# Six loads of a scan-and-adapter kernel, each issued as two transfers of unequal row counts

## The chip, the core and the metric

The kernel runs on one core of a Trainium2 chip. The core has a matrix engine (PE, with weight loads shown as PEld), a vector engine (DVE), an activation engine (ACT), a general engine (POOL), a sequencer that issues transfers (SP), and 16 DMA engines that move data between the chip's memory (HBM) and the on-chip memory (SBUF, 128 partitions). The metric is the device time of one execution in microseconds; lower is better. Before the change the median of three runs is 204.86 us (204.76 to 204.96).

## The reference

First a linear recurrence along time, one for each of 8 batches and 128 channels, then a mixture of eight small adapters on each of its 51,200 output rows, with the two largest gates out of eight:

```python
for t in range(S):                       # S = 6400, arrays (8, 6400, 128), float32
    h = a[:, t] * h + b[:, t]
    out[:, t] = h
...
logits = x @ w_gate                      # x: (51200, 128), w_gate: (128, 8)
topk = np.argpartition(-logits, K, axis=1)[:, :K]      # K = 2
...
z = x[mask] @ A[e]                       # (128, 16)
delta[mask] += w[mask, k, None] * (z @ B[e])
...
return (x + delta).astype(np.float32)
```

## The kernel before

**Tiling.** The 51,200 rows are cut into 100 units of 512 rows (`UT`). For each unit w, PE transposes a and b (`AB{w}`, into PSUM tiles pA and pB), ACT copies pA to SBUF (`aev{w}`, tile a_st), DVE runs the scan over 512 time steps (`scan{w}`, output xT, 128 channels on the partitions). Then come the logits (`L`), the products with all eight adapters' A side by side (`Z`), their weighting by the gates (`mul`, on DVE, some on POOL), a transpose back (`T`, `tev`), and the sum of x and the product with B in PSUM tile pO (`R`, `D`). `oev{v}` (line 789) copies pO into one of 24 slots of the SBUF tile outt, on ACT, in the last ten units on ACT or DVE. The gates themselves are worked out for groups of one to four units (`gating`), mostly on POOL.

**Transfers.** Loads and stores are all issued on SP, by `add_dma` (line 306 holds the `dma_start`). One load brings two neighbouring units of a or of b: 128 rows of 4 KB, one row for each partition, 512 KB in all. Row p of the load holds 8 consecutive time steps, so the lower 64 partitions hold one unit and the upper 64 the other. Only the loads of a0, b0, b1 and a99 bring one unit (256 KB, rows of 2 KB). The loads of a start at the odd units, those of b at the even ones. a_in and b_in are rings of eight such loads; a load into a slot waits until the units that used it have been transposed. 49 stores write two units each (512 KB) and two write one (256 KB). A store waits for the copies of its units, and up to unit 75 also for the scan 20 units later (`HOLD`, `FREE`), so stores trail behind.

**Landing.** Every transfer adds 16 to a semaphore of its slot; `add_dma` counts 16 for each transfer in its list `starts` and the users wait for the sum. So a load of two transfers is used when both have landed.

**Order.** `_Plan.schedule` is a planner in the host program: it simulates the engines with the costs that are written beside each operation, takes at each step the engine that can go on soonest, and on it the ready operation with the smallest key (its unit plus an offset for its kind). The result is a fixed order of instructions for each engine. For a transfer it takes 450 ns on SP for each `dma_start`, then a time on a link that transfers share one after the other: 1265 ns for a load of two units. `load` (line 417) gives a load the key w - 16, so loads go ahead of stores when both are ready.

**What the change touches.** The call of `add_dma` inside `load`, whose fourth argument is the list of transfers, and a new table of constants at the top.

Of the kernel before, what the change touches and what calls it, by code (L numbers as in the profile page):

```python
# [20 lines left out]
POOL_MULS = (0, 20, 4, 2)  # L21
HOLD = 20
FREE = 96
RING = 8
XR = 16
NOUT = 24
# [60 lines left out]
class _Plan:  # L87
# [9 lines left out]
    def add(self, name, eng, kind, unit, cost, emit, deps=(), dma=None, bank=None, mode=None):  # L97

        engs = (eng,) if isinstance(eng, str) else eng
        cost = cost if isinstance(cost, dict) else {e: cost for e in engs}  # L100
        self.ops[name] = _Op(name, engs, kind, unit, cost, emit, list(deps), dma, bank, mode)
# [98 lines left out]
def bass_associative_scan_2x2__then__mixture_of_adapters_kernel(  # L200
# [20 lines left out]
    lo, hi, every, at = POOL_MULS  # L221
# [23 lines left out]
    with ExitStack() as stack:  # L245
# [11 lines left out]

        a_in = sb(nc.sbuf_tensor("a_in", [128, RING, QI * D], F32))
        b_in = sb(nc.sbuf_tensor("b_in", [128, RING, QI * D], F32))
        a_st = [sb(nc.sbuf_tensor(f"a_st{i}", [128, UT], F32)) for i in range(2)]  # L260
# [36 lines left out]
        def add_dma(name, eng, unit, starts, slot, time, deps=()):  # L297

            if slot not in dma_sem:
                dma_sem[slot] = [sb(nc.semaphore("q_" + "_".join(map(str, slot)))), 0]  # L300
            dma_sem[slot][1] += 16 * len(starts)
            sem, value = dma_sem[slot]

            def emit(h):
                for dst, src in starts:
                    last = h.dma_start(dst, src).then_inc(sem, 16)
                return last

            add(name, eng, "dma", unit, (450.0 * len(starts), 0.0), emit, deps, (sem, value, time))
# [91 lines left out]
        def place(t, w):  # L401

            shift = 1 if t == "a" else 0
            half = 64 * ((w + shift) % 2)
            return (w + shift) // 2, slice(half, half + 64)
# [7 lines left out]
        def column(t, w):  # L413

            return w * UT if t == "b" else 0

        def load(t, w):

            n = place(t, w)[0]
            many = 1 if (t, w) in alone else 2  # L420
            dst, i = rings[t][:, n % RING, :], QI
            if many == 1:
                dst, i = dst[:, column(t, w) : column(t, w) + UT], Q
            src = rows_of[t][w * UT : (w + many) * UT, :].rearrange("(p i) d -> p (i d)", i=i)
            for k in range(many):
                load_of[t, w + k] = f"ld{t}{w}"
            add_dma(
                f"ld{t}{w}",
                "sp",
                w - 2 * RING + (0 if w > 3 else -200),  # L430
                [(dst, src)],
                (t, n % RING, many, w if many == 1 else 0),
                650.0 if many == 1 else 1265.0,
                users.get((t, n - RING), []),
            )
# [369 lines left out]
        def store(j):  # L805
# [9 lines left out]
                632.0 * n,  # L815
                [f"oev{v}" for v in range(u0, u0 + n)] + [f"scan{u0 + HOLD}"] * (u0 + HOLD < FREE),
            )

        for w in range(NU):
            for t in "ab":  # L820
                if (t, w) not in load_of:
                    load(t, w)
# [69 lines left out]
```

## Time and profile before

| | |
|---|---|
| median of the runs | 204.86 us |
| the profiled execution | 204.77 us |
| its span, first to last instruction | 203.0 us |
| granted clock of PE, mean | 0.982 |
| moved by DMA | 79.35 MB, 391 GB/s over the span |
| read from HBM, written | 52.56 MB, 26.21 MB |
| loads of 512 KB, a and b | 49 and 49, 13.6 and 13.4 us from issue to landing (median) |
| stores of 512 KB | 49, 13.2 us (median) |

How to read the views. A stretch row gives, for a window of the execution, the busy time and the number of instructions of each engine, PE's granted clock, the mean share in which the 16 DMA engines were busy, and what they moved. A timeline row gives start, length, engine, line, operation and tiles; "SPq" is the issue of a transfer, not the transfer. A row by tile gives the shortest, median and longest duration in ns and the first and last start, and a line below it the time from issue to the landing of all of a transfer. A wait row names who waited, for whom, for how long in total, how often, and the longest.

Both kinds of work run all the time: PE is busy for 93% of the span, and the 16 DMA engines are at or above nine tenths in all but the first and the last few of 40 slices. Latencies of 13 us for a transfer whose bytes take 1.3 us on 16 engines say that some ten transfers stand in the queues.

### The profile page before, as it was taken

How to read it: one execution, taken by the hardware profiler on the slowest of the kernel's cores; microseconds unless marked ns; L12 is line 12 of the kernel's file. 1: busy time of each engine (PE TensorE's matmuls, PEld its weight loads, DVE VectorE, ACT ScalarE, POOL GpSimd, SP SyncE). 2: the span in 40 equal slices, each digit the busy share in tenths (PEclk: the TensorE clock that was granted, in tenths of full speed). 3: DMA queues.
4: the chain of work that ended last, by engine and by line, in shares of the span. 5: the costliest groups of instructions: out<-in, count | busy, mean ns of one | idle time of the engine just before them, and what ended most of it. 6: DMA issues, size and time to landing. Idle time of an engine off the chain costs nothing.

```text
span 203.0 us, 8739 instructions
## 1 busy us (share of the span) xinstructions
PE 189.5 (93%) x3594; PEld 167.2 (82%) x3594; DVE 183.8 (91%) x260; ACT 172.8 (85%) x379; POOL 115.4 (57%) x240
## 2 busy tenths in 40 slices
PE   7788899998999999999999999999999999999970
PEld 2567788887889989988899889999998999889960
DVE  1599988999999999999999999999999999999960
ACT  2357498896979999999999999999999999898870
POOL 1326767655758565646656665575775654555610
PEclk9999699999999999999999999999999999999996
DMA  7999999999999999999999999999999999999884
GB/s 184 403 408 407 406 409 402 405 407 408 407 410 413 408 413 416 404 411 408 412 408 415 408 410 409 408 413 411 410 410 411 408 414 409 400 403 358 319 318 151
DMA packets 29671, 79.35 MB, mean 391 GB/s; under 512 B 3648, under 2 KB 3776, under 8 KB 29632
## 3 DMA queue, kind: packets, MB, share of 16 engines
q1 hardware_dynamic: 28304, 78.65, 98.3%
q8 instruction: 29, 0.48, 0.9%
q10 hardware_dynamic: 1328, 0.14, 0.5%
q14 instruction: 10, 0.08, 0.1%
HBM read 52.56 MB, written 26.21 MB: 388 GB/s over the span
## 4 chain that ended last, share of the span: by engine, by line
PE 85%; ACT 7%; DVE 2%; issue 2%
PE pA L81 28%; PE pO L77 22%; PE pTL L81 14%; PE pZ L77 11%; PE pTL L77 5%; PE pB L81 4%; ACT a_st L474 3%; PE pB L77 2%; DVE xT L493 2%; ACT zwT L750 2%; ACT outt L789 2%; ACT z_sb L698 1%; DVE outt L789 0%; ACT g L667 0%; DVE warm_t L355 0%
## 5 line engine op out<-in xcount | busy, mean ns | idle before, releaser
L493 DVE TENSOR_TENSOR_SCAN xT<-a_st,xT,pB 128x512 f16<-128x512 f32 x96 | 120.2, 1252 | 4.5 <-PE pTL L77 1.0
L474 ACT COPY a_st<-pA 128x512 f32<-128x512 f32 x100 | 60.9, 609 | 19.0 <-PE pB L81 15.3
L81 PE MATMUL pA<-ident_f,a_in 64*128 64x64 f32 (+1 forms) x792 | 72.1, 231 | 2.8 <-ACT a_st L474 1.2
L81 PE MATMUL pB<-ident_f,b_in 64*128 64x64 f32 (+1 forms) x792 | 72.6, 231 | 0.2
L81 PEld LDWEIGHTS pA<-ident_f,a_in 64*128 64x128 f32 (+1 forms) x792 | 58.0, 140 | 12.6 <-ACT a_st L474 2.9
L789 ACT COPY outt<-pO 128x512 f32<-128x512 f32 x95 | 59.6, 628 | 1.6 <-PE pO L77 1.4
L81 PEld LDWEIGHTS pB<-ident_f,b_in 64*128 64x128 f32 (+1 forms) x792 | 58.1, 140 | 0.7 <-issue 0.5
L750 ACT COPY zwT<-pTL 128x512 f16<-128x512 f16 x95 | 58.0, 611 | 0.2
L712 DVE TENSOR_TENSOR zw<-pZ,g 128x512 f16<-128x512 f32 x80 | 53.5, 672 | 0.8 <-PE pTL L81 0.2
L77 PE MATMUL pO<-ident_h,xT 128*128 128x128 f16 x400 | 38.6, 220 | 0.7 <-issue 0.3
L77 PE MATMUL pZ<-cst_h,xT 128*128 128x128 f16 x400 | 38.8, 221 | 0.1
L81 PE MATMUL pTL<-ident_h,zw 128*128 128x128 f16 x380 | 38.0, 223 | 0.5 <-issue 0.3
L77 PE MATMUL pO<-cst_h,zwT 128*128 128x128 f16 x400 | 38.1, 217 | 0.3 <-ACT zwT L750 0.3
L712 POOL TENSOR_TENSOR zw<-z_sb,g 128x512 f16<-128x512 f32 x20 | 21.3, 1063 | 17.2 <-PE pTL L77 15.0
L77 PEld LDWEIGHTS pO<-ident_h,xT 128*128 128x128 f16 x400 | 27.8, 114 | 1.8 <-issue 0.6
L77 PE MATMUL pTL<-cst_h,xT 128*128 128x8 f16 x400 | 27.2, 174 | 1.8 <-DVE xT L493 1.8
L77 PEld LDWEIGHTS pZ<-cst_h,xT 128*128 128x128 f16 x400 | 28.2, 114 | 0.4 <-issue 0.3
L81 PEld LDWEIGHTS pTL<-ident_h,zw 128*128 128x128 f16 x380 | 21.9, 98 | 7.0 <-ACT zwT L750 0.7
L77 PEld LDWEIGHTS pTL<-cst_h,xT 128*128 128x128 f16 x400 | 23.3, 116 | 2.7 <-DVE xT L493 2.2
L608 POOL TENSOR_TENSOR d<-Lg,m 128x128 f32<-128x128 f32 (+3 forms) x29 | 10.8, 374 | 25.1 <-DVE m L601 25.1
L77 PEld LDWEIGHTS pO<-cst_h,zwT 128*128 128x128 f16 x400 | 24.0, 97 | 0.9 <-PE pO L77 0.6
L643 POOL TENSOR_SCALAR pn<-d 128x128 f32<-128x128 f32 (+3 forms) x31 | 17.5, 565 | 2.7
(35 smaller groups left out, 137.0 us busy)
## 6 DMA issues: line engine op xcount, KB each, us to landing
a_in<-in_a_dram SPq DMA_DIRECT2D x49, 512.0 KB, 13.6
b_in<-in_b_dram SPq DMA_DIRECT2D x49, 512.0 KB, 13.4
out_dram<-outt SPq DMA_DIRECT2D x49, 512.0 KB, 13.2
a_in<-in_a_dram SPq DMA_DIRECT2D x2, 256.0 KB, 8.0
b_in<-in_b_dram SPq DMA_DIRECT2D x2, 256.0 KB, 4.2
out_dram<-outt SPq DMA_DIRECT2D x2, 256.0 KB, 4.6
cst_f<-in_moe_A_dram ACTq DMA_DIRECT2D x1, 64.0 KB, 3.9
cst_f<-in_moe_B_dram ACTq DMA_DIRECT2D x1, 64.0 KB, 5.0
```

The costliest lines, as they stand in the source:

```text
L77: return self.h.matmul(*args, **kw)
L81: return self.h.transpose(*args)
L474: lambda h: h.copy(a_st[w % 2][:, :], pA[0][:, :]),
L493: last = h.tensor_tensor_scan(out=x_at(lo, hi), data0=a_st[w % 2][:, lo:hi], data1=pB[w % 2][:, lo:hi], initial=init, op0=ALU.mult, op1=AL ...
L608: lambda h: h.tensor_tensor(out=v(d1[s]), in0=v(Lg[s]), in1=bc(m1[s]), op=ALU.subtract),
L643: lambda h: h.tensor_scalar(v(pn[s]), v(d2[s]), 0.0, -1.0e30, ALU.is_lt, ALU.mult),
L698: lambda h: h.copy(src[:, :], pZ[v % NZ][:, :]),
L712: lambda h: h.tensor_tensor(out=oview, in0=zview, in1=gview, op=ALU.mult),
L750: lambda h: h.copy(zwT[v % 2][:, :], t_dst(v)),
L789: return copy(outt[:, v % NOUT, :], pO[v % NO][:, :])
```

## The change

A table names six loads by tensor and first unit and gives a number of rows. Each of these loads is issued as two transfers, first the rows up to that number and then the others, into the same places; the bytes, the ring slots and what waits for the load stay the same. The semaphore of the load now counts 32, and the planner takes 900 instead of 450 ns on SP for it, with the same 1265 ns on the link.

| load | units | rows | issued before at (us) |
|---|---|---|---|
| b 26 | 26, 27 | 120 + 8 | 25.25 |
| a 45 | 45, 46 | 120 + 8 | 58.45 |
| b 64 | 64, 65 | 120 + 8 | 94.46 |
| b 88 | 88, 89 | 104 + 24 | 141.87 |
| a 91 | 91, 92 | 88 + 40 | 147.15 |
| b 94 | 94, 95 | 120 + 8 | 153.63 |

```diff
@@ -21,6 +21,7 @@
 POOL_MULS = (0, 20, 4, 2)
 HOLD = 20
 FREE = 96
+FIRST_ROWS = {("b", 26): 120, ("a", 45): 120, ("b", 64): 120, ("b", 88): 104, ("a", 91): 88, ("b", 94): 120}
 RING = 8
 XR = 16
 NOUT = 24
@@ -424,11 +425,13 @@
             src = rows_of[t][w * UT : (w + many) * UT, :].rearrange("(p i) d -> p (i d)", i=i)
             for k in range(many):
                 load_of[t, w + k] = f"ld{t}{w}"
+            first = FIRST_ROWS.get((t, w))
+            starts = [(dst[lo:hi], src[lo:hi]) for lo, hi in ((0, first), (first, 128))] if first else [(dst, src)]
             add_dma(
                 f"ld{t}{w}",
                 "sp",
                 w - 2 * RING + (0 if w > 3 else -200),
-                [(dst, src)],
+                starts,
                 (t, n % RING, many, w if many == 1 else 0),
                 650.0 if many == 1 else 1265.0,
                 users.get((t, n - RING), []),
```

## The prediction

> **What bounds the kernel now.** I read the page first, for the share of each engine, then the DMA share by stretches, then the waits, then the last issues on SP.
>
> ```profile
> span 203.0 us, 8739 instructions
> PE 189.5 (93%) x3594; PEld 167.2 (82%) x3594; DVE 183.8 (91%) x260; ACT 172.8 (85%) x379; POOL 115.4 (57%) x240
> ```
>
> PE and DVE are nearly full, so the middle of the run belongs to compute. The stretches show the DMA side (columns: stretch, length, busy time of the engines, granted clock, DMA share, GB/s):
>
> ```profile
> core 0: us, PE busy (x) PEld busy (x) DVE busy (x) ACT busy (x) POOL busy (x), PEclk, DMA share, GB/s
> 65.00:165.00 100.00, 99.47 (x2009) 90.20 (x2007) 97.88 (x129) 96.05 (x210) 62.58 (x112) 1.00 1.04 411
> 182.00:197.00 15.00, 14.52 (x236) 13.06 (x230) 13.68 (x24) 12.91 (x29) 7.53 (x21) 1.00 0.88 333
> 197.00:199.90 2.90, 0.06 (x2) 0.00 (x0) 0.00 (x0) 0.59 (x1) 0.00 (x0) 0.85 0.97 364
> 199.90:201.69 1.79, 0.00 (x0) 0.00 (x0) 0.00 (x0) 0.00 (x0) 0.00 (x0) 0.50 0.07 25
> 201.69:202.97 1.28, 0.00 (x0) 0.00 (x0) 0.00 (x0) 0.00 (x0) 0.00 (x0) 0.50 0.00 0
> ```
>
> From 65 to 165 us all 16 DMA engines are busy; full occupation reads 1.04 here, since records of neighbouring packets overlap a little. So one engine alone reads 1.04 / 16 = 0.065 and moves 411 / 16 = 25.7 GB/s. That is exactly what stands from 199.90 to 201.69: 0.07 and 25 GB/s. **One DMA engine works on alone for 1.79 us** after the other fifteen have stopped, and the kernel waits for it. Between 182 and 197 us the share is already 0.88 of 1.04: 15% of 16 engines for 15 us, some 37 us of engine time, lies idle, while this one engine has a backlog. The bytes are even, since every transfer gives each engine an equal part; this engine is simply late.
>
> That compute doesn't set the end follows from the last copy and the last stores:
>
> ```profile
> 197.10 0.59 ACT L789 COPY outt<-pO 128x512 f32<-128x512 f32 x1 [0.56 <-PE pO L77]
> ```
> ```profile
> L306 SPq DMA_DIRECT2D out_dram<-outt x1: 344/344/344, 197.7 to 197.7; - x1
> DMA to landing us min/median/max: 4.4/4.4/4.4
> ```
> ```profile
> L306 SPq DMA_DIRECT2D a_in<-in_a_dram x1: 381/381/381, 0.7 to 0.7; - x1
> DMA to landing us min/median/max: 2.9/2.9/2.9
> ```
>
> The last copy ends at 197.69, its store is issued at once and lands 4.4 us later, at 202.1. A transfer of the same 256 KB, issued at 0.7 us with nothing ahead of it, lands in 2.9. So 1.5 us of the last store's latency is backlog; by the stretches it is 1.79, which I use, as a load is not a store.
>
> Loads bind nobody after the start. The only wait for one in the whole table of waits is
>
> ```profile
> PE pA L81 <- DMA a_in<-in_a_dram: 0.2, 1, 0.2
> ```
>
> **The change, part by part.** Six loads of 128 rows (4 KB a row) become two transfers each; the bytes stay. An even transfer gives each of 16 engines 128 / 16 = 8 rows. I take it that a part of 120, 104 or 88 rows still goes in eights, on 15, 13 or 11 engines, and that the rest of 8, 24 or 40 rows goes evenly over 8, 12 or 10 engines, 1, 2 or 4 rows each. A row takes 4096 B / 25.7 GB/s = 0.159 us of one engine, eight of them 1.28 us.
>
> If the engines used are always the same ones from one end of the row of sixteen, the sums over the six are: one engine (left out by all six) loses 48 rows, -7.6 us; two lose 16 rows, -2.5 us each; one loses 8 (-1.3), one loses 6 (-1.0); the other eleven gain 2 to 10 rows, +0.3 to +1.6 us (eight of them gain 10).
>
> *The end.* If the engine that is late is the one left out, its 7.6 us are over four times the 1.79 us that it is late by; two splits would do. It then stops with the others. What is late next is the fifteen: they stop at 199.90, and the last store was issued at 197.7, which no DMA engine can change. Landing, the final wait and the end of the program follow as now, 1.28 us from the last packet to the end of the span. New span: 199.90 + 1.28 = 201.2, that is -1.8 us.
>
> *The eleven that gain.* Up to 1.6 us each, nearly all of it ahead of 165 us. The idle 37 us between 182 and 197 cover it for most: 37 / 15 = 2.5 us each on average. Without that cover an engine that had no idle time would stop at 199.90 + 1.6 = 201.5, almost where the late one stops now. I take 0.1 us for the forecast and keep 1.6 as the other end.
>
> *Issue on SP.* Six more instructions of L306. Their price lies between the rows of a free and of a full queue:
>
> ```profile
> 60.52 0.33 SPq L306 DMA_DIRECT2D b_in<-in_b_dram  x1
> 147.15 2.93 SPq L306 DMA_DIRECT2D a_in<-in_a_dram  x1
> ```
>
> The second one is the very load of units 91 and 92, and its long time is back-pressure from full queues: total DMA work isn't changed, so such a stall moves rather than grows. Behind it on SP stand the next load and the next store. I take 0.33 to 1 us apiece, at the issue only. Who could feel it: PE, by a load, or ACT, by a slot of outt that isn't stored yet. For the load of 91:
>
> ```profile
> L81 PE MATMUL pA<-ident_f,a_in x724: 221/223/366, 5.0 to 166.2; 64*128 64x64 f32 x180, 128*128 128x128 f32 x1
> ```
> ```profile
> DMA to landing us min/median/max: 14.9/14.9/14.9
> ```
>
> It is issued at 147.2 and lands at 162.1. The 724 transposes of a that start up to 166.2 are 4 + 8 x 90, units 0 to 90, so unit 91 is read later than that: over 4 us of margin against, at most, 4 more rows (0.64 us) plus one issue. If that cover were gone, PE would lose the excess directly. ACT never waits for a store in the table of waits. Near the end SP issues as soon as a copy is done, so nothing that it lost before is still felt there: this copy ends at 185.40, and its store goes at 185.42.
>
> ```profile
> 184.76 0.64 ACT L789 COPY outt<-pO 128x512 f32<-128x512 f32 x1
> ...
> 185.42 12.64 SPq L306 DMA_DIRECT2D out_dram<-outt x8
> ```
>  Price on the path: 0, worst case 6 x 0.33 = 2 us if every added issue reached the end.
>
> *The planner.* It counts 900 instead of 450 ns for these six on SP. Its loads end by the line for the transfers, whose total is the same 1265 ns, so the orders of PE, DVE, ACT and POOL should stay as they are; at most a load and a store change places on SP. Price 0; the bound is again the margin of 4 us.
>
> Sum against the profiled execution: 204.77 - 1.79 + 0.1 = 203.1. The median of the runs is 204.86, 0.09 above it; I leave the sum at **203.1**.
>
> What decides is which engine is late, and no view of the profile numbers the engines. What speaks for the one left out is that the lateness is one engine's, not spread: fifteen stop within 0.4 us of each other,
>
> ```profile
> 199.50:199.90 0.40, 0.00 (x0) 0.00 (x0) 0.00 (x0) 0.00 (x0) 0.00 (x0) 0.50 0.69 256
> 199.90:201.60 1.70, 0.00 (x0) 0.00 (x0) 0.00 (x0) 0.00 (x0) 0.00 (x0) 0.50 0.07 25
> ```
>
> and a lateness that belongs to one engine's place is likelier at an end of the sixteen than inside. I hold that for a little better than even. What adds unequal work at present are instruction fetches, one engine at a time: 29 of 16 KB,
>
> ```profile
> q8 instruction: 29, 0.48, 0.9%
> ```
>
> 0.9% of 16 x 203 us over 29 is 1.0 us each; one fetch more than the others alone makes an engine late by 1.0 us.
>
> The Trainium skill, "DMA: Bandwidth & Descriptors", section "Why a DMA increments its semaphore by 16 and not by 1", says that such a transfer uses the largest number of engines, up to 16, that divides its rows, always the lowest-numbered ones: by it the last engine is left out by all six, as in my sum, while no run here shows an uneven transfer yet. Its section "Latency and other measured facts" calls engines 7 and 15 usually slower in traces, which would be the last one (203.1) or one of the eight that gain ten rows (the third rival).
>
> **The rivals.**
>
> *Partly.* The late engine goes, but one of those that gain has no idle time and sets the end: between 203.1 and 201.5 + 1.28 + 1.77 (from span to time: 204.77 - 203.0) = 204.6, middle 203.9. For it: between 197.0 and 199.9 the share is 0.97 of 1.04, so few engines idle there. Against it: the 37 us before.
>
> *The wrong engine.* The late engine is one of the eleven that gain rows. Place: its queue, from the first split on; it is never idle, so every row shows at the end: +0.3 us (2 rows) to +1.6 us (10 rows), most likely the latter. Time 204.9 + 1.6 = 206.5, slower than before. It decides as soon as the late engine isn't among the five relieved. For it: five of sixteen are relieved, and only three by over 1.79 us. Against: the argument on the end of the row, above.
>
> *Two engines at one door.* In an even transfer every engine writes its own set of partitions; with other counts the sets shift, and two engines may write the same part of the memory, at half the pace. Place: the packets of the split loads; price up to 1.28 us per split on each engine, 7.6 us for six, half of it where engines are out of step: 3.8 + 1.6 - 1.79 = +3.6 us, 208.5. It decides from about 3.5 us of such loss. Against: the 0.97 and 1.04 of the rows above show no slow pace, but they hold even transfers only. The Trainium skill, "SBUF — State Buffer", section "Door 1: The DMA port swizzle (why `[64,N]` ≈ `[32,N]`)", gives the mapping of partitions to 16 ports by which 8 neighbouring partitions lie on two ports; no run so far shows it.
>
> *Nothing.* The division into engines isn't by eights, all sixteen still share each part, and the late one stays late: 204.9. The Trainium skill, "DMA: Bandwidth & Descriptors", section "Rules for kernel authors", calls two transfers to disjoint halves of the partitions not worth the while, since both spread over all 16 engines; that would be this case, and the traces of even transfers can't decide it.
>
> **How the numbers follow.** Forecast 0.54; partly 0.14; wrong engine 0.19; one door 0.05; nothing 0.08. Differences under 0.2% (0.4 us) can't be told from none here. Faster: 0.54 + 0.12 = 0.66. Same: 0.08 + 0.01 = 0.09. Slower: 0.19 + 0.05 and 0.01 of the rest = 0.25. The forecast's own range is 202.6 to 203.6; the range of 8 in 10 goes from 202.6 through "partly" and "nothing" into the milder half of "wrong engine", 206.0, which leaves out about 0.15.
>
> **What would show it.** Right: after the last copy the DMA share drops from about 1 to 0 at once, without a stretch of 0.07 alone; the last store lands in 2.5 to 3 us instead of 4.4; the last copy still ends near 197.7; PE, DVE and ACT keep their busy times. Wrong engine: the stretch at 0.07 grows to over 3 us. One door: packets of loads slower in the stretches after 25 and 58 us, a share of 1.04 at under 400 GB/s, and waits of PE for loads. Partly: several engines late, a share of 0.13 or more at the end. The prediction fails altogether if the last copy moves by over 0.5 us, for then the planner's order changed.

## The result, and the profile after

| | before | changed |
|---|---|---|
| median of the runs | 204.91 us (4 runs, 204.76 to 205.03) | 215.35 us (4 runs, 214.33 to 216.88) |
| the profiled execution | 204.77 us | 214.33 us |
| its span | 203.0 us | 212.5 us |
| granted clock of PE, mean | 0.982 | 0.968 |

The ratio is 1.052 (95% interval 1.045 to 1.058): the change makes the kernel slower by 5%, where I had forecast 0.9% faster. The profiled execution of the changed kernel is the fastest of its four, so what follows accounts for its 9.5 us of span and not for the 10.4 between the medians.

The page of the changed kernel, first the span, the busy times, the DMA share and what DMA moved in 40 slices of 5.3 us:

```profile
span 212.5 us, 8745 instructions
PE 190.5 (90%) x3594; PEld 168.2 (79%) x3594; DVE 184.0 (87%) x260; ACT 173.0 (81%) x379; POOL 115.0 (54%) x240
...
DMA  7999999999999999999999999999999999999991
GB/s 195 402 405 409 408 406 402 233 390 407 407 412 414 342 409 408 410 410 411 410 337 392 412 405 404 410 410 414 406 339 344 327 328 385 395 395 389 356 346 49
```

The engines do the same work in the same time (PE 190.5 against 189.5 us, DVE 184.0 against 183.8); the 9.5 us are idle time. The DMA engines are busy in all but the last slices, as before. But what they move drops in four places: to 233, 342 and 337 GB/s in one slice each, and to about 330 in four slices in a row. These are the places of the split loads, some ten microseconds after their issue. So it isn't that DMA had nothing to do; it took longer for the same bytes.

The stretches around those drops in both kernels. First the kernel before, with one more row that experiment 4 needs:

```profile
core 0: us, PE busy (x) PEld busy (x) DVE busy (x) ACT busy (x) POOL busy (x), PEclk, DMA share, GB/s
37.00:43.00 6.00, 5.72 (x118) 5.16 (x118) 6.00 (x10) 5.16 (x12) 2.75 (x5) 1.00 1.03 407
71.00:74.00 3.00, 2.93 (x60) 2.66 (x56) 3.00 (x6) 2.66 (x8) 1.82 (x4) 1.00 1.03 413
107.00:113.00 6.00, 6.00 (x128) 5.46 (x125) 6.00 (x8) 5.79 (x14) 3.44 (x7) 1.00 1.04 410
113.00:153.00 40.00, 39.95 (x806) 36.20 (x805) 39.15 (x53) 38.49 (x85) 25.56 (x45) 1.00 1.03 410
153.00:179.00 26.00, 25.81 (x520) 23.37 (x520) 25.57 (x36) 24.32 (x52) 14.04 (x27) 1.00 1.04 408
```

Then the changed kernel, with a row between two drops (43 to 71 us, at the pace of before) and the end of its span in the last two rows:

```profile
37.00:43.00 6.00, 5.72 (x115) 5.09 (x114) 5.70 (x9) 5.16 (x11) 3.12 (x7) 1.00 1.04 240
43.00:71.00 28.00, 26.11 (x526) 23.39 (x527) 26.94 (x35) 24.16 (x54) 17.39 (x32) 1.00 1.03 408
71.00:74.00 3.00, 2.95 (x62) 2.57 (x60) 3.00 (x6) 2.68 (x8) 1.56 (x4) 1.00 1.05 305
107.00:113.00 6.00, 6.00 (x130) 5.47 (x126) 6.00 (x8) 5.80 (x14) 3.58 (x8) 1.00 1.04 336
153.00:179.00 26.00, 21.76 (x389) 19.57 (x386) 19.75 (x28) 18.81 (x41) 11.11 (x21) 0.87 1.02 342
205.00:207.20 2.20, 0.00 (x0) 0.00 (x0) 0.00 (x0) 0.00 (x0) 0.00 (x0) 0.62 0.90 342
207.20:211.25 4.05, 0.00 (x0) 0.00 (x0) 0.00 (x0) 0.00 (x0) 0.00 (x0) 0.50 0.17 64
```

A share of 1.04 with 240 GB/s is the picture to learn: **the DMA engines are occupied and slow**, as if each packet had to wait at the other end. Single packets do take longer: of the packets of 4 KB that start between 37 and 43 us, the median takes 162 ns before and 294 ns in the changed kernel. Each row can be turned into lost time. Where 407 GB/s were moved before and 240 now, 1 - 240/407 = 41% of 6 us is lost, 2.46 us. The four stretches give 2.46, 0.78, 1.08 and 4.21 us, together **8.5 us**. An engine whose queue never runs empty can't make that up. The prediction had found one such engine. If it is one of those that get ten rows more, 10 x 0.159 = 1.6 us come on top, and 10.1 us stand against 9.5 measured.

That sum is an estimate, for it gives the late engine the mean loss of all sixteen, while the end of the span shows an uneven loss. From 207.20 on 0.17 of 1.04 is the work of some 2.6 engines, for 4 us, where one engine worked for 1.79. Each engine leaves a landing event for its share of a transfer; for the last store these are, in us from the start of the span:

```
before:  15 events from 200.07 to 200.23 | 202.11
changed: 11 events from 207.32 to 207.47 | 207.93 208.30 209.39 210.90 211.67
```

Where one engine was late, five are now. The last is 0.77 us behind the next, where it was 1.87, so some engine lost at least 1.1 us more than the one that was late before.

PE suffers too. Its waits between 155 and 185 us, and the last copy:

```profile
PE pA L82 <- DMA a_in<-in_a_dram: 4.0, 2, 3.4
```
```profile
204.11 0.59 ACT L792 COPY outt<-pO 128x512 f32<-128x512 f32 x1 [0.56 <-PE pO L78]
```

PE, which before waited 0.2 us for loads, now waits 4.0 us for loads of a in this stretch, 3.4 of them at once (4.4 in the whole run). In the row of 153 to 179 us the granted clock is 0.87 instead of 1.00, and the last copy ends at 204.70 instead of 197.69, 7.0 us later. So there are two candidates for what set the end: the DMA queue of the late engine, +9.5 us at the last landing, or PE, +7.0 us at the last copy. The last two stores decide between them only in part:

```profile
L307 SPq DMA_DIRECT2D out_dram<-outt x2: 881/979/1077, 203.8 to 204.7; - x2
...
DMA to landing us min/median/max: 7.0/7.1/7.3
```

The last one lands 7 us after its issue, where it took 4.4 before. On eleven engines it landed 2.6 to 2.8 us after its issue, so these had no backlog left; the last engine needed 4.2 us more than they, though PE's delay gave it 7 us to catch up.

### The profile page after: what moved, and what is told of

Read it like the earlier page. It is cut to its first block, busy times and chain, and to the rows that moved or that the text cites. A ratio compares the mean times of both kernels' runs of the same rounds, so it can differ in the third digit from the quotient of the medians.

```text
span 212.5 us, 8745 instructions
## 1 busy us (share of the span) xinstructions
PE 190.5 (90%) x3594; PEld 168.2 (79%) x3594; DVE 184.0 (87%) x260; ACT 173.0 (81%) x379; POOL 115.0 (54%) x240
## 4 chain that ended last, share of the span: by engine, by line
PE 75%; ACT 8%; DMA 8%; issue 3%; DVE 2%; SPq 0%; DVEq 0%
PE pA L82 25%; PE pO L78 19%; PE pTL L82 13%; PE pZ L78 9%; DMA a_in<-in_a_dram 8%; PE pTL L78 4%; PE pB L82 4%; ACT a_st L477 3%; ACT zwT L753 2%; DVE xT L496 2%; PE pB L78 2%; ACT outt L792 1%; ACT z_sb L701 1%; ACT g L670 0%; DVE outt L792 0%
## 5 line engine op out<-in xcount | busy, mean ns | idle before, releaser
L611 POOL TENSOR_TENSOR d<-Lg,m 128x128 f32<-128x128 f32 (+3 forms) x29 | 10.8, 372 | 27.4 <-DVE m L604 27.3
L639 POOL TENSOR_TENSOR d<-Lg,m 128x128 f32<-128x128 f32 (+3 forms) x29 | 10.8, 373 | 19.0 <-DVE m L632 19.0
```

The source lines that it names most:

```text
L611: lambda h: h.tensor_tensor(out=v(d1[s]), in0=v(Lg[s]), in1=bc(m1[s]), op=ALU.subtract),
L639: lambda h: h.tensor_tensor(out=v(d2[s]), in0=v(Lg[s]), in1=bc(m2[s]), op=ALU.subtract),
```

## The experiments

The theories, as the expectations name them: *doors* or *queue* (packets of split loads, and those beside them, take longer because several engines write the same part of the memory; the late engine's queue carries this to the end), the wrong engine (the late engine gets more rows), SP (the six further issues), and PE (the lost time near the end is PE's). All edits are to the changed kernel unless said.

**1. Same number of transfers, even ones: split by columns.**

```diff
-            starts = [(dst[lo:hi], src[lo:hi]) for lo, hi in ((0, first), (first, 128))] if first else [(dst, src)]
+            starts = [(dst[:, lo:hi], src[:, lo:hi]) for lo, hi in ((0, 512), (512, 1024))] if first else [(dst, src)]
```

> The same six loads are split into two transfers each, but by columns: 128 rows of the first 2 KB, then 128 rows of the second 2 KB. Every engine keeps its own 8 partitions. Theory DOORS (in a part with other row counts two engines write the same part of SBUF, so that their packets and those of the even transfers beside them go at half the pace): no fall of the GB/s in any stretch (over 400 from 37 to 43 us, against 240 in the changed kernel), time 204.9 +- 0.5. Theory TWO TRANSFERS (the second issue and the second landing cost): the time stays near the changed kernel's, 213 to 215. Theory FEWER ENGINES (the loss is the idle of engines that get nothing): 204.9, as doors.

Measured 205.28 us (10 runs, 205.18 to 205.37) against 204.94: ratio 1.0013 (1.0004 to 1.0023). Two of its stretches:

```profile
37.00:43.00 6.00, 5.72 (x120) 5.14 (x119) 6.00 (x9) 5.15 (x12) 2.81 (x5) 1.00 1.03 402
153.00:179.00 26.00, 25.81 (x520) 23.37 (x520) 25.57 (x37) 24.32 (x52) 13.99 (x26) 1.00 1.04 406
```

The drops to 240 and 342 are gone with the rows left whole. The six further issues, and the planner's larger cost for them, cost no more than the 0.3 us that are left (0.5 at the end of the interval). SP is out.

**2. Split by rows, but even on 16 engines: 64 + 64.**

```diff
-FIRST_ROWS = {("b", 26): 120, ("a", 45): 120, ("b", 64): 120, ("b", 88): 104, ("a", 91): 88, ("b", 94): 120}
+FIRST_ROWS = {("b", 26): 64, ("a", 45): 64, ("b", 64): 64, ("b", 88): 64, ("a", 91): 64, ("b", 94): 64}
```

> The same six loads, split by rows into 64 and 64. Each part goes on all 16 engines, 4 rows each, so no engine is left out and none gets more rows than before. DOORS: 64 neighbouring partitions lie behind half of the doors, so two engines share one in each part; stretches of 37 to 43 us and so on fall to 250 to 330 GB/s again, time 209 to 216. FEWER ENGINES or unequal rows: no loss, 204.9 +- 0.5. TWO TRANSFERS: 213 to 215.

Measured 214.54 us (213.39 to 214.65), ratio 1.0467 (1.0449 to 1.0484); its span is 211.6.

```profile
37.00:43.00 6.00, 5.83 (x112) 5.06 (x110) 6.00 (x9) 5.16 (x13) 2.86 (x5) 1.00 1.05 228
71.00:74.00 3.00, 2.94 (x66) 2.65 (x63) 3.00 (x5) 2.67 (x7) 2.19 (x5) 1.00 1.06 324
107.00:113.00 6.00, 6.00 (x124) 5.44 (x124) 5.88 (x10) 5.80 (x14) 4.40 (x8) 1.00 1.03 326
153.00:179.00 26.00, 23.50 (x462) 20.88 (x458) 23.83 (x33) 22.35 (x50) 13.33 (x25) 1.00 1.04 341
```

Here 64 rows divide by 16, so by the division that the prediction assumed no engine is left out and none gets more rows. The drops are all there: 2.64 + 0.65 + 1.23 + 4.27 = 8.8 us by the rows, and the span is 8.6 longer. So the loss doesn't come from the unequal share; it comes from which rows go together in a transfer. The changed kernel's profiled span is 0.9 us longer still, which is the side on which ten further rows of the late engine would put it. It doesn't prove them: here, with no rows added to any, eleven engines land the last store 1.0 to 4.8 us after the first five, so several engines come late without further rows.

**3. and 4. Three of the six at a time.**

```diff
# the first three alone
+FIRST_ROWS = {("b", 26): 120, ("a", 45): 120, ("b", 64): 120}
# the last three alone
+FIRST_ROWS = {("b", 88): 104, ("a", 91): 88, ("b", 94): 120}
```

> Only b26, a45 and b64 are split (120 and 8). DOORS: three falls of the GB/s, as in the changed kernel, 2.4 + 0.8 + 1.1 = 4.3 us of all the DMA engines' time. The margin of the late loads (4.6 us at the least before) shrinks to about 0.3, so PE hardly waits for loads; the lost time comes back in the tail, less what idles there (37 us of engine time, 2.3 us each): 206 to 208. If the split did cost only at the six loads themselves and not in the queue behind them: 204.9.

> Only b88, a91 and b94 are split. DOORS: the fall between 153 and 179 us stays (342 GB/s in the changed kernel, 4.2 us lost), the loads of units 91 to 98, which had 4.6 to 6 us of margin, come about when they are needed; PE waits for loads 0 to 3 us instead of some 8; time 206 to 210. If the two sets simply add, this and the run with the first three add up to +10 us over before; by the margin theory (nothing waits until 4.6 us are lost, then every us counts) the sum of the two is clearly less than +10.

Measured: the first three 209.9 us, ratio 1.0249 (1.0231 to 1.0268), span 207.7; the last three 211.32 us, ratio 1.0317 (1.0300 to 1.0334), span 209.4. The first three alone:

```profile
37.00:43.00 6.00, 5.72 (x120) 5.14 (x118) 6.00 (x9) 5.16 (x11) 3.21 (x6) 1.00 1.04 238
71.00:74.00 3.00, 2.94 (x61) 2.64 (x60) 3.00 (x7) 2.68 (x7) 1.55 (x3) 1.00 1.08 302
107.00:113.00 6.00, 6.00 (x124) 5.44 (x123) 5.87 (x10) 5.79 (x14) 4.38 (x8) 1.00 1.03 333
```

The last three alone:

```profile
113.00:153.00 40.00, 39.90 (x807) 36.26 (x808) 39.11 (x52) 38.45 (x84) 25.48 (x45) 1.00 1.04 403
153.00:179.00 26.00, 24.00 (x475) 21.54 (x473) 23.69 (x33) 22.58 (x50) 13.54 (x25) 1.00 1.03 335
```

I had expected the two to add up to clearly less than the whole, since I thought that the margin of the loads and the idle DMA time near the end would swallow a part of each. Both came out longer than the 206 to 208 and 206 to 210 us that I expected. They come to +5.0 and +6.4, that is 11.3 with the decimals kept, against 10.4 for all six. Nothing is swallowed, not even of a split load issued at 25 us, with 170 us to make up for it. By the rows the first three lose 2.49 + 0.81 + 1.13 = 4.4 us, with three further rows 4.9, and the span grows by 4.7. The last three lose 0.7 + 4.65, with seven further rows 6.4, and the span grows by 6.4.

**5. The transfers by themselves.** A kernel of loads and stores only, all computation left out: groups of seven, each on the partitions named, a wait between the groups.

```python
load("all128", 0, 128); load("low120", 0, 120); load("low64", 0, 64)
load("mid64", 32, 96);  load("mid60", 32, 92);  load("low88", 0, 88)
store("o128", 0, 128, 0);   store("o120", 0, 120, N)
store("o64", 0, 64, 2 * N); store("om64", 32, 96, 3 * N)
```

> Nothing but transfers, all computation is left out: seven loads of 128 rows of 4 KB (partitions 0 to 127), then, each group after the landing of the one before, seven of 120 rows (0 to 119), of 64 rows (0 to 63), of 64 rows (32 to 95), of 60 rows (32 to 91), of 88 rows (0 to 87); then seven stores each of 128, 120, 64 (0 to 63) and 64 (32 to 95) rows. DOORS with the mapping of the skill's page (partitions p and p+32 and 4 neighbours share one of 16 ports): 410 GB/s for 128 rows; 120 rows at half the pace, 190 to 250; 64 rows on 0 to 63 at 200 to 215 and on 32 to 95 at 400; 60 rows on 32 to 91 at 380; 88 rows at 140 to 190. The stores the same by groups. FEWER ENGINES (only the engines left out cost): 120 rows 385, both kinds of 64 rows 400, 60 rows 385, 88 rows 280.

One execution, a stretch in each group, in the order of the code:

```profile
core 0: us, POOL busy (x), PEclk, DMA share, GB/s
5.00:11.00 6.00, 0.00 (x0) 1.00 1.02 402
15.00:29.00 14.00, 0.00 (x0) 1.00 0.95 224
33.00:40.00 7.00, 0.00 (x0) 1.00 0.98 200
43.00:48.50 5.50, 0.00 (x0) 1.00 0.89 295
51.50:55.50 4.00, 0.00 (x0) 1.00 0.92 342
60.00:69.00 9.00, 0.00 (x0) 1.00 0.70 214
73.50:80.00 6.50, 0.00 (x0) 1.00 1.03 407
84.00:92.00 8.00, 0.00 (x0) 1.00 0.90 345
96.00:102.50 6.50, 0.00 (x0) 1.00 0.97 208
106.00:109.00 3.00, 0.00 (x0) 1.00 1.01 406
```

With nothing else on the chip, a load of 120 rows runs at 224 GB/s and one of 128 at 402. Sixty-four rows on partitions 0 to 63 take 16 engines and still run at half pace, 200 for the load and 208 for the store; the same 64 rows on partitions 32 to 95 store at the full 406. So it is neither the number of rows nor the number of engines, but which partitions the engines reach at the same time. The Trainium skill, "SBUF — State Buffer", section "Door 1: The DMA port swizzle (why `[64,N]` ≈ `[32,N]`)", says that within each half of 64 partitions p and p + 32 share one of 16 ports; by it rows 0 to 63 reach eight ports and rows 32 to 95 all sixteen, which agrees with 208 and 406 GB/s. It isn't the whole: the load of rows 32 to 95 ran at 295 (in single microseconds between 201 and 410), where I expected full pace, the 60 rows at 342, also below what I expected, and the 88 rows at 214 above it. A store of 120 rows reaches 345, much more than the load. What the reading direction changes stays open.

**6. and 7. Can the late engine be relieved in stores instead?** In the kernel before, the last two and the last four stores of the run are split 120 + 8, after the point where loads matter.

```diff
-                [(rows, outt[:, s0 : s0 + n, :])],
+                [(rows[lo:hi], outt[lo:hi, s0 : s0 + n, :]) for lo, hi in (((0, 120), (120, 128)) if u0 >= 98 else ((0, 128),))],
# the other: u0 >= 94
```

> The kernel before, with no load split, but the last two stores (256 KB each) issued as 120 and 8 rows. Nothing waits behind them but the end. If the engine that is late at the end (1.8 us) is the one that gets nothing of the 120 rows: it has 16 packets of 2 KB less, -1.28 us, while the others, idle there, take up to 0.7 us longer at the door: 203.6 to 204.2, faster than before. If the late engine is one that takes part in both pieces: 205.0 to 205.6.

> As the run with the last two stores, and the two stores of 512 KB before them as well (units 94 to 99 in all). The late engine would lose 48 packets of 2 KB, 3.8 us, more than its 1.8; the other engines pay the door twice for 1.3 us each, and idle for 0.6 us between two stores: end between 200.5 and 202.5 in the span, time 203.4 to 205.3 if the late engine is the one left out, over 205.5 if not.

Measured 205.31 us, ratio 1.0020 (1.0011 to 1.0029), and 205.62 us, ratio 1.0045 (1.0027 to 1.0063). Both are slower, though each such store takes eight rows from the engine that is left out. If that were the late one, even the two single stores, with 16 rows of half the length, would relieve it by 16 x 0.159 / 2 = 1.3 us. So it is hardly the late one. The landing events of experiment 6 say so directly: of the 23 for the last store, in its two pieces, 21 come up to 201.08 and two at 202.47 and 202.66. So the late engine has a share in both pieces, and the one that is left out would have a share in neither.

**8. One split load, the farthest from the end.**

```diff
+FIRST_ROWS = {("b", 26): 120}
```

> Only b26 is split (120 and 8). DOORS: the stretch from 37 to 43 us falls to 240 GB/s, 2.4 us of all engines lost; by addition with the other two (0.8 and 1.1 us) about half of the +5.0 us of the run with the first three: 207.2 to 207.6. If the cost per split is the same wherever it stands: +1.7, 206.6. If what is lost at 40 us is regained in the idle of the tail: under 205.5.

Measured 207.26 us, ratio 1.0111 (1.0096 to 1.0127), span 205.5.

```profile
37.00:43.00 6.00, 5.89 (x112) 5.11 (x111) 6.00 (x9) 5.16 (x12) 2.91 (x5) 1.00 1.04 241
```
```profile
197.61 0.58 ACT L792 COPY outt<-pO 128x512 f32<-128x512 f32 x1 [0.56 <-PE pO L78]
```

One load at 25 us costs 2.45 us of DMA time at 40 us by this row, with one further row 2.6, and the span is 2.5 us longer 160 us later. The last copy ends at 198.19, only 0.5 us later than before, so the loss doesn't travel by PE; it travels in the DMA queue. Nor is it the split load's alone: between 25 and 60 us 305 packets of 4 KB take over 220 ns, against 16 in the kernel before. The split load has 128 packets, so at least 161 of the slow ones belong to other transfers.

**9. Is there one late engine that sets the end at all?** In the kernel before, the stores of units 76 to 79 are left out, 2 x 8 x 0.159 = 2.5 us of each engine.

```diff
-            store(j)
+            if stores[j][0] not in (76, 78):
+                store(j)
```

> The kernel before with the stores of units 76 to 79 left out (two of 512 KB, 2.56 us on each DMA engine, issued at 175 and 177 us, after the last load). If the late engine sets the end, as the prediction read it, 1.79 us of the 2.56 show and then the last store does: 203.0 to 203.3. If the end hangs on the last copy and its store alone: 204.9.

Measured 203.5 us against 205.02, ratio 0.9926 (0.9912 to 0.9939). Its end, and its last store:

```profile
199.90:200.50 0.60, 0.00 (x0) 0.00 (x0) 0.00 (x0) 0.00 (x0) 0.00 (x0) 0.55 0.67 249
200.50:201.60 1.10, 0.00 (x0) 0.00 (x0) 0.00 (x0) 0.00 (x0) 0.00 (x0) 0.50 0.00 0
```
```profile
L306 SPq DMA_DIRECT2D out_dram<-outt x1: 344/344/344, 198.2 to 198.2; - x1
...
DMA to landing us min/median/max: 2.5/2.5/2.5
```

The stretch with one engine alone is gone, all sixteen landing events of the last store lie within 0.18 us (200.60 to 200.77), and 1.5 us are won; the time lies 0.2 above the 203.0 to 203.3 that I expected. So the first part of the prediction holds: one engine's backlog set the end, and the stake was about the 1.8 us that it was read as.

**10. Which engine is the late one?** In the kernel before, the two single stores of units 98 and 99 are cut into three pieces: 112 rows, which all sixteen engines share, then 7 and 9 rows, or 4 and 12.

```diff
+        cuts = {98: ((0, 112), (112, 119), (119, 128)), 99: ((0, 112), (112, 116), (116, 128))}
-                [(rows, outt[:, s0 : s0 + n, :])],
+                [(rows[lo:hi], outt[lo:hi, s0 : s0 + n, :]) for lo, hi in cuts.get(u0, ((0, 128),))],
```

> The kernel before; the last two stores (units 98 and 99) are issued in three pieces each: 112, 7 and 9 rows, then 112, 4 and 12 rows, which go by the skill's rule on the lowest 16, 7 and 9, and 16, 4 and 12 engines. The late engine's landings come 1 to 2 us after the others'. Late engine among the lowest four: three late landings and three. Among the fifth to the seventh: three and two. The eighth or ninth: two and two. One of the last four: one and one. The theory that the change gives the late engine more rows excludes the last case.

204.98 us, in one run. The last landing events of the two stores, in us from the start of the span:

```
store of unit 98 (112, 7, 9): ... 199.60 199.65 199.77 | 201.41 201.62 201.81
store of unit 99 (112, 4, 12): ... 200.61 200.72 200.78 | 202.12 202.30
```

Each store has 34 events: two at once after the issue, and 16 + 7 + 9 or 16 + 4 + 12, one for each engine that has a share. Late by 1.3 us or more are three events of the first store and two of the second: the late engine has a share in the pieces of 112, 7, 9 and 12 rows and none in the piece of four. If a piece always takes engines from the same end of the row, the late engine is the fifth, sixth or seventh of sixteen. The Trainium skill, "DMA: Bandwidth & Descriptors", section "Why a DMA increments its semaphore by 16 and not by 1", says that the lowest-numbered engines are taken; the counts agree, but these events don't show from which end. By that rule the late one is 4, 5 or 6, counted from 0. Its section "Latency and other measured facts", on which the prediction drew, has 7 and 15 as usually slower in traces, but calls this specific to transfers whose descriptors are made by software; the page of the profile has the transfers here as hardware_dynamic (q1, 98.3%), so it doesn't bear on them. If the changed kernel has the same late engine, it takes part in both transfers of all six loads and gets ten rows more, 1.6 us by the price of a row.

**11. The same rows, cut so that the largest piece lies on the good partitions.**

```diff
-... for lo, hi in ((0, first), (first, 128))] if first else [(dst, src)]
+... for lo, hi in ((32, 96), (0, 32), (96, 128))] if first else [(dst, src)]
```

> The same six loads in three pieces of 64 (partitions 32 to 95), 32 (0 to 31) and 32 rows (96 to 127), on all 16 engines each. DOORS: the 64 middle rows find 16 doors and cost nothing, the 32 others two engines to a door: about half of the loss of the halves (which cost 9.6 us): +3 to +6 us, 208 to 211, and 37 to 43 us at 290 to 350 GB/s instead of 228. If only the number of pieces counts: more than with two pieces, over 214. If unequal rows count: 204.9.

Measured 208.61 us, ratio 1.0177 (1.0161 to 1.0192), span 206.7.

```profile
37.00:43.00 6.00, 5.72 (x118) 5.08 (x115) 6.00 (x8) 5.16 (x13) 3.21 (x6) 1.00 1.04 309
71.00:74.00 3.00, 2.94 (x63) 2.56 (x61) 3.00 (x5) 2.67 (x7) 2.62 (x5) 1.00 1.02 331
107.00:113.00 6.00, 6.00 (x126) 5.44 (x125) 5.86 (x9) 5.80 (x14) 4.29 (x8) 1.00 1.04 389
153.00:179.00 26.00, 25.80 (x517) 23.30 (x515) 25.51 (x35) 24.24 (x54) 13.98 (x26) 1.00 1.04 385
```

Three transfers a load instead of two, and less than half the loss of 64 + 64: 1.44 + 0.60 + 0.31 + 1.47 = 3.8 us by the rows, span +3.7. The number of transfers isn't the cost; the place of the rows is.

**12. Queue or PE at the end of the changed kernel?** The stores of units 76 to 79 are left out, as in 9, this time of the changed kernel.

> The changed kernel with the stores of units 76 to 79 left out, issued after the last load, so that no load and no engine sees it. QUEUE (the last DMA engine's backlog sets the end, PE's 7 us of delay lie under it): -2.6 us, 212.5 to 213.0. PE (the late last copy, at 204.7 instead of 197.7, sets the end): 215.0 to 215.4, as the changed kernel.

Measured 213.62 us (212.70 to 214.42), 1.7 under the changed kernel's 215.35; to the kernel before the ratio is 1.0435 (1.0415 to 1.0454). Its last copy:

```profile
204.18 0.58 ACT L792 COPY outt<-pO 128x512 f32<-128x512 f32 x1 [0.56 <-PE pO L78]
```

The last copy ends at 204.76, where it ended at 204.70; the end still comes 1.7 us earlier. The intervals of the two ratios to the kernel before just touch (up to 1.0454 here, from 1.0452 there), so the landing events of the last store are the better evidence. Fourteen come between 207.16 and 207.31, and then two at 208.95 and 210.03. In both kernels most engines are done 2.4 to 2.8 us after the last copy; the last engine is done 4.2 us after them in the changed kernel and 2.7 here. So PE's lateness isn't what sets the end; DMA's is. The size falls short of the queue theory's 2.6 us by 0.9, in a kernel whose own runs lie 2.5 us apart; why is open.

No version that does all the work beats the kernel before (experiment 9 leaves out four units' stores).

## Why the prediction was wrong

Two steps of the forecast failed. Its sum relieved the late engine by 1.79 us, and experiments 6 and 10 show that this engine isn't the one left out. And it took a row at 0.159 us in even and uneven parts alike, with no term for slower packets, which by the stretch rows cost 8.5 us. Experiments 1, 2, 5 and 11 show that this cost follows from which rows go together in a transfer.

The books close to 0.6 us in six kernels. Loss by the stretch rows, further rows of the late engine at 0.159 us, and the measured growth of the profiled span over 203.0 us:

| kernel | rows of the stretches | further rows | sum | measured |
|---|---|---|---|---|
| one load (8) | 2.45 | 0.16 | 2.6 | 2.5 |
| 32 + 64 + 32 (11) | 3.8 | 0 | 3.8 | 3.7 |
| first three (3) | 4.4 | 0.5 | 4.9 | 4.7 |
| last three (4) | 5.3 | 1.1 | 6.4 | 6.4 |
| halves (2) | 8.8 | 0 | 8.8 | 8.6 |
| the change | 8.5 | 1.6 | 10.1 | 9.5 |

The column of further rows is an estimate. The stretch rows give the mean of sixteen engines, and by the landing events of the changed kernel the loss differs between engines by 1.1 us at least.

**What bounds the kernel: right.** One engine's backlog ends the run, and the stake was 1.5 to 1.8 us (experiment 9). The sharper reading, that the engine is never idle and so every lost microsecond of DMA shows at the end, stood in the prediction only under the rival of the wrong engine. It fits all six kernels of the table.

**"If the engine that is late is the one left out": the step that failed first.** It was chosen from where the lateness is likelier to be, "at an end of the sixteen", with no row behind it. Experiment 6 finds it in both pieces of 120 and 8 rows, and experiment 10, by the rule on the lowest-numbered engines, at the fifth to seventh place, among the eight that gain ten rows. The term of -1.79 us becomes about +1.6 us, an estimate that no run shows by itself. The rival of the wrong engine had this price; its 206.5 us lacks the larger cost.

**"Two engines at one door": right in mechanism, wrong in size and chance.** What I had listed as its mark, a share of 1.04 at under 400 GB/s, is what the rows show (240, 305, 336). I wrote 1.28 us per split and 7.6 us for six, then halved it because engines would be out of step, and gave the whole 0.05. Measured are 8.5 us for six, 1.4 a split. The halving was the mis-sized term: 7.6 + 1.6 without it and without the -1.79 is 9.2 us, against 9.5. That this comes so near is in part luck, since the first three split loads cost 2.46, 0.78 and 1.08 us and not 1.28 each. The single load of experiment 8 lost 2.45 us, about twice what its own rows would lose at half pace. Transfers beside it are slowed too, by the count of slow packets; that they meet the split load's engines at the same places in memory is argued from experiment 5, since no packet's place is on record. The evidence that I held against this rival was the pace of even transfers, which, as I wrote myself, says nothing of uneven ones.

**The eleven that gain, with the idle 37 us as their cover: wrong.** That cover exists for engines that idle. The late engine has none, and the mean loss of all sixteen was 8.5 us, where I had 1.6 us as the bound. The five late events of the last store are also what the rival "partly" had named as its mark, several engines late.

**The margin of the loads: wrong.** "Over 4 us of margin against, at most, 4 more rows (0.64 us) plus one issue" counted the load's own rows. The load of units 91 and 92, for which PE waited 3.4 us, was issued at 154.09 instead of 147.15 and landed at 172.53 instead of 162.03: 6.9 of the 10.5 us were lost before its issue, the other 3.6 behind it. As the prediction put it, PE loses the excess directly; yet it isn't on the path that sets the end (experiment 12), because the DMA queue is later still.

**Issue on SP, priced at nothing: right** (experiment 1, 0.3 us with everything else of two transfers, 0.5 at the end of the interval). **The planner: right.** On every engine the instructions stand in the same order in both kernels, apart from the six added issues on SP. But its mark was wrong: I wrote that a last copy moved by over 0.5 us would mean a changed order. It moved by 7.0 us with the order unchanged, since PE was fed late.

**Open.** Why the second split load costs 0.78 us and the first, with the same 120 + 8 rows, 2.46. Where some idle time of PE near the splits comes from in which it waits for no semaphore. In experiment 3 a gap of 1.04 us stands at 78 us, between transposes of one unit:

```profile
77.74 0.22 PE L82 MATMUL pA<-ident_f,a_in 64*128 64x64 f32 x1
...
79.01 0.27 PE L82 MATMUL pB<-ident_f,b_in 64*128 64x64 f32 x1 [1.04 <-issue]
```

Instruction fetches, which the page lists among the DMA queues, could be late there; this wasn't tried.

## What to carry to other kernels

Read the DMA share beside the GB/s: a share near 1 with fewer bytes meant here that packets took longer, and (1 - pace now / pace before) x length of the stretch is the time lost, which came out at the end here, where one DMA engine's queue never ran empty. Splitting a 128-row transfer by rows cost far more than the rows it moves (64 + 64 on six loads +4.7%), while splitting it by columns cost 0.1%. Before moving work away from a late unit, find out which unit it is: here the landing events of two stores cut into pieces of different counts show it.

## What was not expected of the hardware

- A load of 120 rows alone runs at 224 GB/s and one of 128 at 402; 64 rows at 200 to 208 on partitions 0 to 63, but 406 in a store on partitions 32 to 95.
- A single split load of 512 KB slows the transfers around it as well: 241 GB/s over 6 us, 2.45 us lost, where its own bytes at 407 GB/s take 1.29 us; at least 161 packets of other transfers took over 220 ns instead of 162.
- The direction matters: 120 rows at 224 GB/s into the on-chip memory, 345 out of it; rows 32 to 95 at 295 in, 406 out.
- The late DMA engine isn't the one that an uneven split leaves out (experiment 6), and in experiment 10 its share lies in the pieces of 7, 9 and 12 rows and not in that of 4.
- PE's granted clock was 0.87 between 153 and 179 us of the changed kernel, where PE had waited for loads, and 1.00 in the same stretch before.
